# A fused attention and expert kernel on one core: the second dense group's preparation set later, the gate's last steps held back, two banks and the first loads rearranged

## The chip, the cores and the metric

The kernel runs on one NeuronCore of one Trainium2 chip. The metric is the time of one execution on the device in microseconds (us). TensorE (PE) multiplies, ScalarE (ACT) and VectorE (DVE) read its banks of PSUM and do the elementwise work, GpSimd (POOL) does elementwise work in SBUF and issues gathers and scatters, and SyncE (SP) issues most other transfers. Each engine works through its own instructions in order.

## The reference

Windowed attention, then a layer of eight experts of which each token takes two, then a dense layer with a piecewise gate. All in float32 (the second layer's weights come as float64 in the kernel's inputs and are decoded on the chip).

```python
rel = pos[:, None] - pos[None, :]
scores = np.where((rel >= 0) & (rel < 64), q @ k.T / 8, -1e9)
attn = exp(scores - max) / (sum + 1e-9)
x = (attn @ v)                                  # 2304 tokens x 512
noisy = x @ w_gate + log1p(exp(x @ w_noise)) * noise
top2 = the two largest of 8;  w = softmax over the two
x = sum over the two: w * (relu(x @ w1[e]) @ w2[e])          # 512 -> 1024 -> 512
h = x @ w_in                                                 # 512 -> 2048
g = where(h >= 1, h, where(h <= -1, 0, (h + 1) ** 2 / 4))
out = g @ w_out                                              # 2048 -> 512
```

## The kernel before

The tokens are cut into 18 tiles of 128. **Attention** goes by token tiles. The scores of tile i are two units u = 2i and 2i+1, each a bank of 128x512; units take the three banks `Sb` in turn (u modulo 3). `A` writes a tile's scores: two products with a mask open each bank, 32 products of queries and keys follow. `top` takes the row maxima on VectorE, `soft` the exponentials on ScalarE, `C` transposes the probabilities, and `Dm` multiplies them with the values into `OB`, a tile of two banks. Some filler products (`warm`) also go into `OB`. Before the loop SyncE is given the loads of keys and queries of the first pair of tiles (two halves), then values, then keys and queries of the second pair, then more values.

**Experts.** The tokens of an expert are gathered into tiles of 128 rows, transposed on TensorE (`xpose`, L756) into a bank, and copied out as a high half by ScalarE (L759) and a low half by VectorE (L760), since products run in a reduced form of float32 and three products of halves make one of full precision. A hidden chunk is 128 wide: `mm1` makes it (L885), ReLU leaves it in the hidden tile `hall` as two halves, and `mm2` (L949) adds its share to the output banks. Expert 0 comes in two parts, "0a" and "0b"; while 0b is worked on, the six tiles of the first large expert "e1" are transposed into bank 7, one per chunk, the last two at the same chunk. `tail` finishes the routing meanwhile, and `count` ranks the experts by their number of tokens.

**Dense layer.** The 18 tiles are cut into groups of 2, 4, 4, 4 and 4 (`G2`). The first group runs plainly (`plain`), while the others use a form with seven products of sums for eight (`wino`). In the first group the work goes in eight dense tiles p = 0 to 7, of two hidden chunks f = 0 and 1 each. For TensorE the order is: the first product of tile p+1 (L885, 24 products of 256 columns), then the second product of tile p (L949, 12 of 512 columns). Between lie the steps of `act_gate` for each chunk: ReLU (L903) and a half of it (L904) on ScalarE, two steps on VectorE (L905, L906), the copy into `hall` on ScalarE (L909) and the low half on VectorE (L910). The first product's banks 0 and 1 alternate by chunk.

The second group (called g1) is prepared while the first runs. For each of its four token tiles the two expert outputs y are loaded from `y_dram` through GpSimd's queue once all scatters have landed. They are scaled on ScalarE (L1019) and mixed on VectorE (L1021) in `mix_two`, transposed on TensorE in `xturn` (L1221) and copied by ScalarE in `xcopy` (L1227). `xsums` (L1240) forms the sums, and `split_two` (L1250, L1252) makes the halves of the seven operands. Where these steps stand is written out by hand: `FILL[(p, f)]` hangs steps into the gate of chunk f of tile p, and the main loop at the end of `fused_kernel` puts others between the seven steps j of a second product, by conditions on (p, j). The names y2 to y5 below are the second group's four token tiles, counted over all groups.

Of the kernel before, what the change touches and what calls it, by code (L numbers as in the profile page):

```python
# [11 lines left out]
F32 = mybir.dt.float32  # L12
# [19 lines left out]
NB = 5  # L32
# [25 lines left out]
def fused_kernel(ctx, tc, qT, kT, v, wg, noise, wcat, out, wd=None):  # L58
# [195 lines left out]
    load_qk(0)  # L254
    load_v(0)
    load_qk(1)
# [86 lines left out]

    def A(i):
        j = i // 2
        qo, ko = (i % 2) * P, (i % 2) * P
        sb = [Sb[(2 * i + k) % 3] for k in range(2)]
# [17 lines left out]
    def top(u):  # L365
        mx = wk.tile([P, 4], F32, tag="mx", name=f"mx{u}", bufs=3)
        nb = wk.tile([P, 4], F32, tag="nb", name=f"nb{u}", bufs=3)
        nc.vector.tensor_reduce(out=mx, in_=Sb[u % 3].rearrange("p (g n) -> p g n", g=4), axis=AX.X, op=ALU.max)
# [4 lines left out]
    def soft(u):  # L373
        sb, nb = Sb[u % 3], mxs.pop(u)
# [418 lines left out]
    def tail():  # L793
# [6 lines left out]
        count()  # L800
# [10 lines left out]
    def count():  # L811
# [25 lines left out]
                                in1=tf[:, 0:R].unsqueeze(2).to_broadcast([P, R, E]), op=ALU.is_equal)  # L837
        for a, src in enumerate((src_i, dst_i)):
# [59 lines left out]

    def act_gate(ps, hh, hl, w):
# [3 lines left out]
        nc.scalar.activation(r, ps, AF.Relu, bias=1.0)  # L903
        nc.scalar.activation(m, r, AF.Copy, scale=0.5)  # L904
        nc.vector.scalar_tensor_tensor(out=r, in0=m, scalar=1.0, in1=r, op0=ALU.min, op1=ALU.subtract)  # L905
        nc.vector.scalar_tensor_tensor(out=r, in0=m, scalar=1.0, in1=r, op0=ALU.min, op1=ALU.mult)  # L906
        for x in parts_of:
            next(x)
        nc.scalar.activation(hh, r, AF.Copy, scale=-1.0)  # L909
        nc.vector.scalar_tensor_tensor(out=hl, in0=r, scalar=-1.0, in1=hh.bitcast(F32), op0=ALU.mult, op1=ALU.subtract)  # L910
# [206 lines left out]
    def plain(ui, p):  # L1117
        w = wi[p % WS]
        for f in range(2):
# [6 lines left out]
            mm1_of(key, n, units[ui]["T"], act_gate, units[ui]["m1"], part(0), part(1))  # L1126
        load_in(p + WS)
# [130 lines left out]
    def copy_two(ui, b):  # L1258
        xcopy(ui, b)
        yield  # L1260

    def sums_two(ui, part):
        yield
        xsums(ui, part)

# [15 lines left out]
    for s in range(len(seq)):  # L1281
# [41 lines left out]
        def ahead_xpose():  # L1323
            for x, b, w in ahead:
                if f == (turn_at[b] if ui == WIDE - 1 else w + 2):
                    prep_xpose(x, b, bank[0] if ui == WIDE else TR)
# [48 lines left out]
        if ui == U7B and f:  # L1375
# [6 lines left out]
          {(5, 3): (6,)})  # L1382
    g1 = FIRST2 + 1

    def later(fn, *a):
        return lambda: fn(*a)
    FILL.update({(2, 1): [later(mix_two, units[g1], b) for b in (0, 1)],
                 (3, 0): [later(mix_two, units[g1], b) for b in (2, 3)],
                 (4, 0): [later(split_two, g1, 0), later(split_two, g1, 1)],
                 (4, 1): [later(sums_two, g1, (0, 1))],  # L1390
                 (5, 0): [later(sums_two, g1, (2, 3))],
                 (5, 1): [later(split_two, g1, j) for j in (2, 3)],
# [85 lines left out]
```

## Time and profile before

| | |
|---|---|
| median of 3 runs | 971.39 us (968.99 to 973.98) |
| profiled execution, its own time | 971.69 us |
| its span, first to last instruction | 969.9 us |
| TensorE busy | 944.0 us (97%) |
| VectorE busy | 661.6 us (68%) |
| ScalarE busy | 447.5 us (46%) |
| GpSimd busy | 220.2 us (23%) |
| mean granted TensorE clock | 0.994 |

The profile is one execution. A row of the order in time has the start, the duration, the engine, the line of the program, the operation, out<-in by the program's names without buffer numbers, the shapes, and in brackets how long the engine stood idle before it and what ended that. PEld is the weight load, which overlaps PE. SPq is SyncE's queue. Granted clock 1.00 means 2.4 GHz, 0.50 means 1.2 GHz.

### The profile page before, as it was taken

What the parts mean: (1) busy time and instruction counts of PE and PEld (TensorE: products, weight loads), DVE (VectorE), ACT (ScalarE), POOL (GpSimd) and SP (SyncE); (2) the same over time, 40 slices, a digit from 0 to 9 for tenths busy, and PEclk for the clock granted to TensorE, in tenths of its full rate; (3) what the DMA queues carried; (4) which work ended last, traced back from release to release, by engine and by line L of the source; (5) the groups of instructions that cost most, each with busy time, mean ns of one, the idle gap of its engine ahead of it and who ended that gap; (6) DMA issues with size and microseconds to landing.
All of it is one profiled execution on the core that took longest, in us unless ns stands there. A gap on an engine that the chain in (4) does not pass through costs nothing. (4 is left out here: it accounts for less than half of the span.)

```text
span 969.9 us, 18052 instructions
## 1 busy us (share of the span) xinstructions
PE 944.0 (97%) x6781; PEld 834.8 (86%) x6781; DVE 661.6 (68%) x1388; ACT 447.5 (46%) x920; POOL 220.2 (23%) x273
## 2 busy tenths in 40 slices
PE   8998999999999999999999997999999999999998
PEld 6886878988898989889888886898999889889897
DVE  4689565378997968889543365766766677577664
ACT  6897324345555555555432355334334333443222
POOL 3221113132634354254402130013002201300000
PEclk9999999999999999999999998999999999999999
DMA  8874125445878878757727574684576558546531
GB/s 249 296 266 144 56 97 187 178 167 192 291 257 290 260 244 278 254 196 251 252 82 239 178 234 159 200 298 155 174 249 230 173 174 295 165 161 214 189 106 44
DMA packets 91274, 196.95 MB, mean 203 GB/s; under 512 B 7320, under 2 KB 18072, under 8 KB 91184
## 3 DMA queue, kind: packets, MB, share of 16 engines
q1 hardware_dynamic: 83152, 171.68, 53.6%
q0 software_dynamic: 6736, 21.86, 6.3%
q10 hardware_dynamic: 1296, 2.23, 0.6%
q8 instruction: 54, 0.88, 0.4%
q14 instruction: 36, 0.29, 0.1%
HBM read 155.45 MB, written 40.29 MB: 202 GB/s over the span
## 5 line engine op out<-in xcount | busy, mean ns | idle before, releaser
L949 PE MATMUL bank<-wo,hall 128*128 128x512 f32 x864 | 239.5, 396 | 0.0
L949 PE MATMUL bank<-w,hall 128*128 128x512 f32 (+3 forms) x944 | 236.0, 398 | 1.4 <-DVE hall L896 1.3
L949 PEld LDWEIGHTS bank<-w,hall 128*128 128x128 f32 (+3 forms) x944 | 168.4, 184 | 37.0 <-DVE hall L896 1.7
L949 PEld LDWEIGHTS bank<-wo,hall 128*128 128x128 f32 x864 | 147.8, 190 | 17.5
L893 ACT ACTIVATE hall<-bank 128x288 fp32r<-128x288 f32 (+6 forms) x128 | 54.0, 422 | 223.3 <-PE bank L885 204.1
L885 PE MATMUL bank<-xhie,w 128*128 128x288 f32 (+4 forms) x768 | 123.0, 302 | 1.6 <-DVE hall L896 1.5
L885 PEld LDWEIGHTS bank<-xhie,w 128*128 128x128 f32 x768 | 113.9, 189 | 9.1 <-DVE hall L896 3.4
L896 DVE SCALAR_TENSOR_TENSOR hall<-bank,hall 128x288 fp32r<-128x288 f32 (+7 forms) x168 | 59.8, 391 | 87.2 <-ACT hall L893 78.5
L149 DVE TENSOR_TENSOR w<-raw,w 128x1024 fp32r<-128x1024 f32 (+1 forms) x71 | 82.4, 1160 | 24.4 <-ACT w L158 20.5
L1163 PEld LDWEIGHTS bank<-xb,wi 128*128 128x128 f32 x576 | 80.4, 188 | 11.5 <-DVE wg L1148 1.2
L1187 ACT ACTIVATE hall<-cg 128x512 fp32r<-128x512 f32 x64 | 40.3, 629 | 100.5 <-DVE cg L1185 100.5
L1163 PE MATMUL bank<-xb,wi 128*128 128x256 f32 x576 | 84.8, 283 | 1.8 <-ACT r L903 0.8
L1163 PEld LDWEIGHTS bank<-xc,wi 128*128 128x128 f32 x480 | 67.2, 188 | 7.6 <-DVE wg L1148 0.6
L1030 POOL TENSOR_TENSOR y<-y,y 128x512 f32<-128x512 f32 x14 | 19.1, 1363 | 227.2 <-ACT y L1029 227.2
L1163 PE MATMUL bank<-xc,wi 128*128 128x256 f32 x480 | 70.2, 281 | 0.2
L158 ACT ACTIVATE w<-raw 128x1024 fp32r<-128x1024 f32 (+1 forms) x71 | 69.3, 976 | 0.0
L885 PE MATMUL bank<-xloe,w 128*128 128x288 f32 (+4 forms) x384 | 69.0, 301 | 0.0
L204 POOL TENSOR_TENSOR td<-rawd 128x512 f32<-128x512 f32 x32 | 33.3, 1039 | 140.7 <-DVE rawd L202 78.2
L1181 ACT ACTIVATE mg<-cg 128x512 f32<-128x512 f32 x64 | 40.1, 626 | 47.1 <-DVE cg L1153 45.4
L1182 DVE SCALAR_TENSOR_TENSOR cg<-mg,cg 128x512 f32<-128x512 f32 x64 | 47.0, 734 | 18.8 <-ACT mg L1181 18.8
L885 PEld LDWEIGHTS bank<-xloe,w 128*128 128x128 f32 x384 | 58.0, 188 | 0.0
L1191 DVE SCALAR_TENSOR_TENSOR hall<-cg,hall 128x512 fp32r<-128x512 f32 x64 | 45.9, 718 | 9.1 <-ACT hall L1187 8.7
(279 smaller groups left out, 1443.5 us busy)
## 6 DMA issues: line engine op xcount, KB each, us to landing
wi<-w1o SPq DMA_DIRECT2D x56, 1024.0 KB
raw<-wcat SPq DMA_DIRECT2D x64, 512.0 KB
rawd<-wd SPq DMA_DIRECT2D x32, 512.0 KB
w1o<-so SPq DMA_DIRECT2D x64, 256.0 KB
y<-y_dram SPq DMA_DIRECT2D x28, 256.0 KB
vE<-v SPq DMA_DIRECT2D x18, 260.0 KB
x_dram<-x SPq DMA_DIRECT2D x18, 256.0 KB
k<-kT SPq DMA_DIRECT2D x8, 512.0 KB
```

Source lines behind the costliest of these rows:

```text
L149: nc.vector.tensor_tensor(out=w[:, 1, c], in0=t[:, c], in1=w[:, 0, c].bitcast(F32), op=ALU.subtract)
L158: nc.scalar.activation(w[:, 0, c], t[:, c], AF.Copy)
L204: nc.gpsimd.tensor_tensor(out=t, in0=hf, in1=lf, op=ALU.add)
L885: nc.tensor.matmul(ps, lhsT=l[k], rhs=r[:, k, s:s + w], start=(c == 0), stop=(c == len(prods) - 1))
L893: nc.scalar.activation(hh, ps, AF.Relu)
L896: nc.vector.scalar_tensor_tensor(out=t, in0=ps[:, c], scalar=0.0, in1=hh[:, c].bitcast(F32), op0=ALU.max, op1=ALU.subtract)
L949: nc.tensor.matmul(M2[b][0:w], lhsT=h2[:, o:o + w], rhs=r[n], start=(first and a == 0), stop=(last and a == end))
L1163: nc.tensor.matmul(ps, lhsT=w[:, l, k * P:k * P + P], rhs=r[:, m, k, :], start=(c == 0), stop=(c == len(prods) - 1))
L1181: nc.scalar.activation(st["m"], c, AF.Relu, scale=0.5)
L1182: nc.vector.scalar_tensor_tensor(out=c, in0=st["m"], scalar=1.0, in1=c, op0=ALU.min, op1=ALU.subtract)
L1187: nc.scalar.activation(h2[:, 0:T], c, AF.Copy, scale=-1.0)
L1191: nc.vector.scalar_tensor_tensor(out=h2[:, T:2 * T], in0=c, scalar=-1.0, in1=h2[:, 0:T].bitcast(F32), op0=ALU.mult, op1=ALU.subtract)
```

## The change

Six things, all of them in the order or the place of work; no arithmetic is added or taken away.

1. The keys and queries of the second pair of tiles are loaded ahead of the first values.
2. The second unit of the second token tile (u = 3) puts its scores into the first bank of `OB` instead of `Sb[0]`.
3. `count` gains a yield before its last part, and `tail` passes it on.
4. The last two steps of `act_gate` (ScalarE's copy into `hall`, VectorE's low half) are held in a list and issued by `close_gate` behind the next chunk's ReLU; behind the last tile they are issued at once.
5. The sixth tile of e1 is transposed into bank 4 instead of bank 7.
6. The second dense group is prepared later: mixing in tiles 3 and 4 instead of 2 and 3, transposes and copies in the second products of tiles 3 and 4 instead of 2, sums in tile 4's, splits in tiles 5 to 7.

```diff
     load_qk(0)
+    load_qk(1)
     load_v(0)
-    load_qk(1)
...
+    def score(u):
+        return OB[:, 0, :] if u == 3 else Sb[u % 3]
...
-        sb = [Sb[(2 * i + k) % 3] for k in range(2)]
+        sb = [score(2 * i + k) for k in range(2)]
...
+    held_gate = []
+
+    def close_gate():
+        for r, hh, hl in held_gate:
+            nc.scalar.activation(hh, r, AF.Copy, scale=-1.0)
+            nc.vector.scalar_tensor_tensor(out=hl, in0=r, scalar=-1.0, in1=hh.bitcast(F32), op0=ALU.mult,
+                                           op1=ALU.subtract)
+        held_gate.clear()
...
         nc.scalar.activation(r, ps, AF.Relu, bias=1.0)
+        close_gate()
...
+        held_gate.append((r, hh, hl))
         for x in parts_of:
             next(x)
-        nc.scalar.activation(hh, r, AF.Copy, scale=-1.0)
-        nc.vector.scalar_tensor_tensor(out=hl, in0=r, scalar=-1.0, in1=hh.bitcast(F32), op0=ALU.mult, op1=ALU.subtract)
...
+        if p == NPR - 1:
+            close_gate()
...
-                    prep_xpose(x, b, bank[0] if ui == WIDE else TR)
+                    prep_xpose(x, b, bank[0] if ui == WIDE else bank[4] if ui == WIDE - 1 and b == NB else TR)
...
-          {(5, 3): (6,)})
+          {})
+    TURN, COPY = {(3, 0): (0,), (3, 1): (1,), (3, 6): (2,), (4, 0): (3,)}, {(3, 3): (0, 1), (4, 2): (2, 3)}
...
-    FILL.update({(2, 1): [later(mix_two, units[g1], b) for b in (0, 1)],
-                 (3, 0): [later(mix_two, units[g1], b) for b in (2, 3)],
-                 (4, 0): [later(split_two, g1, 0), later(split_two, g1, 1)],
-                 (4, 1): [later(sums_two, g1, (0, 1))],
-                 (5, 0): [later(sums_two, g1, (2, 3))],
-                 (5, 1): [later(split_two, g1, j) for j in (2, 3)],
-                 (6, 0): [later(split_two, g1, j) for j in (4, 5)]})
+    FILL.update({(3, 0): [later(mix_two, units[g1], 0)],
+                 (3, 1): [later(mix_two, units[g1], 1)],
+                 (4, 0): [later(mix_two, units[g1], b) for b in (2, 3)],
+                 (5, 0): [later(split_two, g1, j) for j in (0, 1)],
+                 (6, 0): [later(split_two, g1, j) for j in (2, 3)],
+                 (6, 1): [later(split_two, g1, j) for j in (4, 5)],
+                 (7, 0): [later(split_two, g1, 6)]})
...
+                    for b in TURN.get((p, j), ()):
+                        xturn(ui + 1, b)
+                    for b in COPY.get((p, j), ()):
                         xcopy(ui + 1, b)
+                    if p == 4 and j > 4:
+                        xsums(ui + 1, (0, 1) if j == 5 else (2, 3))
```

How the instructions stand now is shown at three places. A row has the line, the operation, out<-in with buffer numbers, and the shape.

ScalarE, the gates of the first group where y is scaled, before (r and m are a chunk's gate, r_7017 is chunk 1 of tile 2, r_7056 chunk 0 of tile 3):

```order
L903 ACTIVATE r_7017<-bank1_74 128x256
L904 ACTIVATE m_7018<-r_7017 128x256
L1019 ACTIVATE y2_6963<-y2_6963,wts_189 128x512
L1019 ACTIVATE y3_6966<-y3_6966,wts_189 128x512
L909 ACTIVATE hall_2150<-r_7017 128x256
L903 ACTIVATE r_7056<-bank0_73 128x256
L904 ACTIVATE m_7057<-r_7056 128x256
L1019 ACTIVATE y4_6970<-y4_6970,wts_189 128x512
L1019 ACTIVATE y5_0_6974<-y5_0_6974,wts_189 128x512
L909 ACTIVATE hall_2150<-r_7056 128x256
```

And now (r_7050 is chunk 0 of tile 3, r_7072 its chunk 1, r_7109 chunk 0 of tile 4; L916 is the ReLU, L907 the held copy):

```order
L916 ACTIVATE r_7050<-bank0_73 128x256
L907 ACTIVATE hall_2150<-r_7015 128x256
L918 ACTIVATE m_7051<-r_7050 128x256
L1032 ACTIVATE y2_6961<-y2_6961,wts_189 128x512
L916 ACTIVATE r_7072<-bank1_74 128x256
L907 ACTIVATE hall_2150<-r_7050 128x256
L918 ACTIVATE m_7073<-r_7072 128x256
L1032 ACTIVATE y3_6964<-y3_6964,wts_189 128x512
L916 ACTIVATE r_7109<-bank0_73 128x256
L907 ACTIVATE hall_2150<-r_7072 128x256
L918 ACTIVATE m_7110<-r_7109 128x256
L1032 ACTIVATE y4_6968<-y4_6968,wts_189 128x512
```

y2 moved by one chunk, y3 to y5 by two, and each copy into `hall` now stands behind the next chunk's ReLU and no longer behind a y of its own chunk.

TensorE, where the y tiles are transposed, before (wo2 is the weight of tile 2's second product, wi0 that of tile 4's first):

```order
L885 MATMUL bank1_74<-xlog0_6798,wi3_6554 128x256 x4
L1221 MATMUL bank7_78<-idn_164,y2_6963 128x128 x4
L949 MATMUL bank2_75<-wo2_6739,hall_2150 128x512
L1221 MATMUL bank4_2142<-idn_164,y3_6966 128x128 x4
L949 MATMUL bank2_75<-wo2_6739,hall_2150 128x512 x2
L949 MATMUL bank3_76<-wo2_6739,hall_2150 128x512 x3
L949 MATMUL bank2_75<-wo2_6739,hall_2150 128x512 x2
L1221 MATMUL bank5_77<-idn_164,y4_6970 128x128 x4
L949 MATMUL bank2_75<-wo2_6739,hall_2150 128x512
L949 MATMUL bank3_76<-wo2_6739,hall_2150 128x512
L1221 MATMUL bank6_2143<-idn_164,y5_1_6975 128x128 x4
L949 MATMUL bank3_76<-wo2_6739,hall_2150 128x512 x2
```

And now (the rows above these hold the whole second product of tile 2 and the first product of tile 4; y5 follows after the first product of tile 5):

```order
L889 MATMUL bank1_74<-xlog0_6798,wi0_6347 128x256 x4
L1236 MATMUL bank7_78<-idn_164,y2_6961 128x128 x4
L962 MATMUL bank2_75<-wo3_6774,hall_2150 128x512
L1236 MATMUL bank4_2142<-idn_164,y3_6964 128x128 x4
L962 MATMUL bank2_75<-wo3_6774,hall_2150 128x512 x2
L962 MATMUL bank3_76<-wo3_6774,hall_2150 128x512 x3
L962 MATMUL bank2_75<-wo3_6774,hall_2150 128x512 x3
L962 MATMUL bank3_76<-wo3_6774,hall_2150 128x512
L1236 MATMUL bank5_77<-idn_164,y4_6968 128x128 x4
```

The transposes moved down by one second product and one first product of a dense tile.

ScalarE at the group's start, before (r_6882 is chunk 1 of tile 0, y7b the last expert's outputs, wo6 and wo7 weight splits, r_6932 chunk 0 of tile 1):

```order
L904 ACTIVATE m_6883<-r_6882 128x256
L909 ACTIVATE hall_2150<-r_6882 128x256
L966 ACTIVATE y7b_0_6896<-bank4_2142 128x512
L955 ACTIVATE y7b_2_6909<-bank6_2143 32x512
L1111 ACTIVATE wo6_6914<-wr6_6777 128x1024
L1111 ACTIVATE wo7_6917<-wr7_6816 128x1024
L903 ACTIVATE r_6932<-bank0_73 128x256
```

And now (r_6880 is chunk 1 of tile 0, r_6930 chunk 0 of tile 1):

```order
L918 ACTIVATE m_6881<-r_6880 128x256
L979 ACTIVATE y7b_0_6894<-bank4_2142 128x512
L968 ACTIVATE y7b_2_6907<-bank6_2143 32x512
L1124 ACTIVATE wo6_6912<-wr6_6777 128x1024
L1124 ACTIVATE wo7_6915<-wr7_6816 128x1024
L916 ACTIVATE r_6930<-bank0_73 128x256
L907 ACTIVATE hall_2150<-r_6880 128x256
```

The copy of tile 0's chunk 1 into `hall` moved from ahead of the two evictions to behind the two weight splits and the next ReLU; VectorE's low half moved in the same way.

## Rows read from the trace of the kernel before

**Rows 1.** What TensorE waited for, whole span: us in total, times, longest us.
```profile
PE bank L1221 <- DVE y L1021: 5.5, 1, 5.5
PE bank L352 <- ACT p L377: 1.9, 2, 1.0
PE bank L756 <- DVE xloe L760: 1.8, 2, 1.5
```

**Rows 2.** Order in time, first dense group, ScalarE's y and TensorE's transposes.
```profile
581.61 0.72 ACT L1019 ACTIVATE y<-y,wts 128x512 f32<-128x512 f32 x1 [2.48 <-DMA y<-y_dram]
...
585.06 0.72 ACT L1019 ACTIVATE y<-y,wts 128x512 f32<-128x512 f32 x1 [2.73 <-DMA y<-y_dram]
...
587.26 1.12 PE L1221 MATMUL bank<-idn,y 128*128 128x128 f32 x4 [5.53 <-DVE y L1021]
...
587.85 0.72 ACT L1019 ACTIVATE y<-y,wts 128x512 f32<-128x512 f32 x1 [0.37 <-DMA y<-y_dram]
...
594.48 1.07 PE L885 MATMUL bank<-xhig,wi 128*128 128x256 f32 x8
```

**Rows 3.** Stretches: their us, busy us by engine, granted clock, DMA share, GB/s.
```profile
170.00:171.00 1.00, 1.00 (x4) 0.79 (x3) 0.45 (x2) 0.95 (x1) 0.00 (x0) 0.50 0.13 53
...
585.00:586.00 1.00, 0.00 (x0) 0.00 (x0) 0.00 (x0) 0.94 (x3) 0.00 (x0) 1.00 1.03 381
...
591.00:592.00 1.00, 1.00 (x3) 0.73 (x3) 0.66 (x2) 0.27 (x1) 0.00 (x0) 0.50 0.00 0
```

**Rows 4.** Order in time, TensorE from expert 0b to the first large expert.
```profile
160.83 0.46 PE L756 MATMUL bank<-idr,xge 128*128 128x128 f32 x4
161.13 1.63 PE L949 MATMUL bank<-w,hall 128*128 128x512 f32 x6
162.59 1.10 PE L885 MATMUL bank<-xhi0b,w 128*128 128x256 f32 x8
...
169.08 0.50 PE L756 MATMUL bank<-idr,xge 64*128 64x64 f32 x4 [1.46 <-DVE xloe L760]
...
174.49 1.44 PE L885 MATMUL bank<-xhie,w 128*128 128x352 f32 x8
...
176.41 1.56 PE L949 MATMUL bank<-w,hall 128*128 128x512 f32 x6
```

**Rows 5.** Order in time, first 15 us; last, a wait of SyncE's queue.
```profile
9.13 0.41 PE L352 MATMUL bank<-mask,id 64*64 64x512 bf16 x2 [0.95 <-ACT p L377]
...
10.93 0.51 SPq L108 DMA_DIRECT2D qbuf<-qT  x1
...
11.03 0.60 ACT L386 ACTIVATE pt<-bank 128x512 f32<-128x512 f32 x1 [0.92 <-PE bank L384]
...
12.71 0.40 PE L352 MATMUL bank<-mask,id 64*64 64x512 bf16 x2 [0.94 <-ACT p L377]
...
14.50 0.27 PE L398 MATMUL ob<-vE__120,pt 128*64 128x65 f32 x1
...
SPq L409 <- DMA qbuf<-qT: 0.9, 1, 0.9
```

**Rows 6.** Order in time, start and end of the first dense group.
```profile
565.38 2.02 PE L949 MATMUL bank<-w,hall 128*128 128x512 f32 x8
...
568.36 0.58 ACT L966 ACTIVATE y7b<-bank 128x512 f32<-128x512 f32 x1
...
570.07 2.92 PE L949 MATMUL bank<-wo,hall 128*128 128x512 f32 x12
...
570.54 2.36 DVE L1112 TENSOR_TENSOR wo<-wr,wo 128x1024 fp32r<-128x1024 f32 x2 [0.27 <-ACT wo L1111]
...
574.48 1.00 PEld L885 LDWEIGHTS bank<-xhig,wi 128*128 128x128 f32 x8 [0.28 <-ACT r L903]
...
615.85 0.97 PE L1163 MATMUL bank<-xb,wi 128*128 128x256 f32 x6 [0.79 <-ACT r L903]
...
617.93 0.98 PE L1163 MATMUL bank<-xb,wi 128*128 128x256 f32 x6 [0.64 <-ACT sg L1144]
```

More of the change, by code (lines that the diff above doesn't have):

```diff
@@ L367, in top @@
         nb = wk.tile([P, 4], F32, tag="nb", name=f"nb{u}", bufs=3)
-        nc.vector.tensor_reduce(out=mx, in_=Sb[u % 3].rearrange("p (g n) -> p g n", g=4), axis=AX.X, op=ALU.max)
+        nc.vector.tensor_reduce(out=mx, in_=score(u).rearrange("p (g n) -> p g n", g=4), axis=AX.X, op=ALU.max)
         (nc.vector if u < 4 else nc.gpsimd).tensor_scalar(out=nb, in0=mx, scalar1=-0.125, scalar2=None, op0=ALU.mult)
@@ L373, in soft @@
     def soft(u):
-        sb, nb = Sb[u % 3], mxs.pop(u)
+        sb, nb = score(u), mxs.pop(u)
         p = wk.tile([P, 4, P], F32, tag="p", name=f"p{u}", bufs=4)
@@ L799, in tail @@
         prep_gather(units[1], 0)
-        count()
+        yield from count()
         rte.close()
@@ L837, in count @@
                                 in1=tf[:, 0:R].unsqueeze(2).to_broadcast([P, R, E]), op=ALU.is_equal)
+        yield
         for a, src in enumerate((src_i, dst_i)):
@@ L1256, in xsplit @@
             pass
[L1258 to L1264, printed above, removed]
     SPLITS = {0: [int(F0 <= f < F0 + NF - EW) for f in range(NF)], 1: [0] + [1] * (NF - 1),
@@ L1431, in fused_kernel @@
                         xcopy(ui + 1, 2 * (p - 2) + j // 2)
-                elif p == 2:
-                    if j in (0, 1, 5, 6):
-                        xturn(ui + 1, j if j < 2 else j - 3)
-                    for b in {3: (0, 1), 6: (2, 3)}.get(j, ()):
+                else:
+                    for b in TURN.get((p, j), ()):
+                        xturn(ui + 1, b)
+                    for b in COPY.get((p, j), ()):
                         xcopy(ui + 1, b)
+                    if p == 4 and j > 4:
+                        xsums(ui + 1, (0, 1) if j == 5 else (2, 3))
                 for x in AT[late].get((p, j), ()):
```

## The prediction

> **What bounds the kernel now.** I read the waits of TensorE first, then the order in time around its long waits, then the granted clock there. The page shows TensorE busy nearly throughout, so what can be won lies in the few places where it stands idle or runs slowly. The list of its waits names them [rows 1]: one of 5.5 us for a token tile y, mixed on VectorE, two for the exponentials, together 1.9, and two for the low half of a transposed tile, together 1.8, of which one is 1.5.
>
> The long one is in the first dense group. The y tiles of the second group are loaded from GpSimd's queue, after the last scatter. ScalarE takes the first at 581.61, the second at 585.06 and the last at 587.85, each when it lands [rows 2]. ScalarE works in order, so all that stands behind these tiles waits too; TensorE reaches the first transpose of y 5.53 us before it can run it, at 587.26. The idle time is not the whole price. The granted clock was still full between 585 and 586, but 0.50 from 591 to 592: it had gone from 2.4 to 1.2 GHz [rows 3]. The next dense tile's first product, at 594.48, comes late on both counts.
>
> The same shows on a smaller scale at the first expert [rows 4, 3]: its last two tiles are transposed into one bank, the second waits 1.46 us for VectorE to empty it, and the clock is 0.50 from 170 to 171. At the kernel's start [rows 5] the second token tile's scores wait 0.95 us for a bank that ScalarE still reads. ScalarE then idles 0.92 us, to 11.03, before the first copy of transposed probabilities.
>
> **The change part by part.** The sum is made against the profiled execution's own 971.69 us, which stands 0.3 above the median of 971.39.
>
> *Last transpose of the first expert, into bank 4.* The wait of 1.46 goes: bank 4 is free there, since the expert that uses it has been evicted and the next writes it only after this tile is copied. The slow stretch: from 169.08 to 174.49 are 5.41 us, for one short transposition, six products of 512 columns and twelve of 352. At full clock these took 0.30 (160.83 to 161.13), 1.46 (161.13 to 162.59) and 1.92 (174.49 to 176.41), so 3.68 [rows 4]. Lost to the clock: 1.73. Term: **-3.19**. What is late next is the copy pair of the last tile on ScalarE and VectorE; both can now run right behind the fifth tile's, while TensorE has six products of 1.46 us to do. Bounds: 1.46 (the clock falls all the same) to 3.19.
>
> *Second group prepared about one dense tile later.* The same transposes, mixes, copies and splits run, none more, none fewer; SyncE's and GpSimd's queues keep their order there, so the tiles land as before. In the order above the first scaling of y now stands behind the ReLU of dense tile 3, and the first transpose behind the products of tile 4. Without the stall TensorE needs about 5.9 us from 581.73 (587.26 less 5.53) to get there (twelve products of 512, 2.92, and tile 4's 24 of 256, about as long), so 587.6. The second y lands at 585.06 and needs a scaling and a mix of about 0.7 each (ScalarE's took 0.72), 586.5: a margin of 1.1. The fourth has until tile 5 is multiplied, over 6 us more, against 587.85. Therefore the 5.53 goes. Slow clock: from 587.26 to 594.48 are 7.22 us for four transposes (1.2) and twelve products (2.92), so 3.10 lost. Term: **-8.63**. Bounds: if the y tiles come 2 us later than now, TensorE waits 0.9 us and may slow again (1.7), so -6.0; nothing more is there to win.
>
> *The held gate.* The last two steps of a chunk's gate (ScalarE's copy into the hidden tile, VectorE's low half) now stand behind the next chunk's ReLU. That frees the score bank sooner, and the 0.28 us that TensorE waited for a ReLU at 574.48 goes [rows 6]: **-0.28**. Against it: the second chunk of each tile is closed only after the next tile's first chunk is multiplied. TensorE multiplies that tile before it consumes the closed chunk, and consumes the other chunk first (six products, 1.46), so there is room. It is tightest at the first tile, where two evictions and two weight splits stand between. As they ran before, VectorE's splits end at 572.90 (570.54 and 2.36) and the low half behind them would end at 573.3; TensorE starts on that tile at 570.07 and is due there eight products later, at 572.0: 1.3 late. But ScalarE took the first of these evictions at 568.36, behind the gate's copy that now stands after it, though TensorE was done with the tiles to evict by 567.4 (565.38 and 2.02) [rows 6]. That brings evictions and splits forward by 1 to 1.5 us. I take the wait as nothing, since the two are about equal; the bound above is 1.3, and 1.7 more with a slow clock behind it.
>
> At the end of the group TensorE waits 0.79 and 0.64 us, for the last ReLU and for the first copy of the next form of product [rows 6]. The first goes, since the ReLU is now ahead of the chunk before it. The second grows by as much, since the last chunk's chain of five steps is no shorter and a split of x (about 0.7 on each engine, as the scaling of y) has moved in ahead of it. Taken as nothing; bounds -0.8 to +0.6.
>
> *Second tile's late scores in a value bank.* TensorE need not wait the 0.95 at 9.13. ScalarE then has its next work as soon as the exponentials of the first tile end (10.11), against 11.03: at most 0.92 sooner. I take 0.75, since the scores must still be transposed and copied in turn. The following tile's wait of 0.94 at 12.71 stays, since it is for ScalarE, and moves with it. The first value products write the same bank, at 14.50 now, 13.75 then; the exponentials that read it end as much sooner. Between here and the first expert no long wait stands in rows 1, so a start that is earlier stays earlier. Term: **-0.75**; bounds 0 and -0.92.
>
> *Second keys and queries ahead of the values.* Two loads move ahead of two others in SyncE's queue. SyncE had issued the next queries by 11.44 (10.93 and 0.51) and then waited 0.9 us on the second queries [rows 5]: they landed at about 12.34. The third tile's scores want them at about 12.0 after the edit above, so without the swap a third of a microsecond is lost again. The values land at 12.34 at the latest if the four together take what they took, and are first read at 13.75. The third keys and queries are issued up to 1.3 us later, some 10 us ahead of use. Nothing of its own; it keeps the term above whole. The Trainium skill, page "DMA: Bandwidth & Descriptors", section "Queues, rings and completion order", says that a queue's descriptors are consumed in ring order on each engine, but that a later one may finish before an earlier one. By its first half the term stays 0.75; by its second the queries may still come at 12.34 and it would be 0.4, the sum 959.2.
>
> *The rest.* The new yield in the counting routine moves no row on any engine: nothing.
>
> Sum: 3.19 + 8.63 + 0.28 + 0.75 = 12.85, so 971.69 - 12.85 = **958.8 us**.
>
> **The rivals.** *The clock falls at the end of the group instead.* The two waits there become one of about 1.5 us, as long as the one at the first expert, behind which the clock fell (1.73 lost). For it: the length. Against it: 1.43 us in two pieces left the clock at full today. It would give 958.8 + 1.7 = 960.5. The Trainium skill, page "TensorE: Matmul & The Clock Gate", Part 1, says that slow is the default, that activity lifts it, and that where the change falls differs from run to run; by that rule equal waits may end differently, and 960.5 would be as likely as 958.8. The rows alone, one fall behind a wait in one piece and none behind two short ones, I read as 0.18.
>
> *The wait moves and doesn't go.* The y tiles land later than now, since TensorE, no longer stalled, has the next weights ordered sooner; the margin of 1.1 at the second transpose is used up. At 2 us late: 0.9 of wait and 1.7 of slow clock, 961.4. Against it: the weights of that step are ordered at about 587.5, when all but the last tile are in.
>
> *Values late.* The first value products wait for their tile, which now stands behind 1 MB of keys and queries. At 1.5 us late the early term turns to +0.75: 960.3.
>
> *Slower: the held gate is late at every tile.* If VectorE's closing half ends after TensorE has done the first six products and two more, TensorE waits in each of the eight dense tiles. From 1.6 us each (8 x 1.6 = 12.8) this eats the gain; at 2.0 with the clock halved twice it gives 958.8 + 16 + 3.4 = 978. For it: at the first tile there is no margin. Against it: from the second on no weight split stands between, and the closing is due 2.9 us after the ReLU's bank is ready, for about 1.3 us of work.
>
> **How the numbers follow.** Forecast 0.60; clock at the group's end 0.18; wait moved 0.10; values late 0.07; slower 0.02; a start or an expert term that isn't kept (961 to 967) 0.03. The range runs from 955.8 (the group's end also gains, and runs differ by about 2 either way) to 963.5, which takes in the first three rivals with the same spread. About 0.5%, 4.9 us, is what a measurement of this kernel can tell from no change; faster by more means under 966.5. Only the last cases miss it, or several at once: faster 0.92, same 0.06, slower 0.02.
>
> **What would show it.** In the profile after: no wait of TensorE for y and none for the low half at the first expert; granted clock 1.00 in the stretches that answer to rows 3; the second tile's scores in one piece, ScalarE's first copy at about 10.1; one wait of some 1.5 us in place of the two at the end of the group. Wrong it would be if a transpose of y still waited, if the clock fell without a wait, or if products on hidden tiles waited for VectorE's closing half.

## The result, and the profile after

| | before | after |
|---|---|---|
| median | 971.39 us (five runs, 968.99 to 973.98) | 957.97 us (five runs, 957.70 to 958.46) |
| profiled execution | 971.69 us | 958.46 us |
| its span | 969.9 us | 956.8 us |
| TensorE busy | 944.0 us | 938.8 us |
| mean granted clock | 0.994 | 1.000 |

The ratio is 0.9864, with a 95% interval of 0.9847 to 0.9881. The forecast was 958.8. Both falls of the clock are gone, and so is most of the spread: the runs of after lie within 0.8 us, those of before within 5.

TensorE's waits after the change (engine, bank and line, what is waited for: total, times, longest) are short:

```profile
PE bank L889 <- DVE hall L900: 1.5, 3, 1.1
PE bank L962 <- DVE hall L900: 1.3, 1, 1.3
...
PE bank L355 <- ACT p L380: 0.9, 1, 0.9
...
PE bank L1178 <- ACT sg L1159: 0.9, 1, 0.9
PE bank L759 <- DMA xg0a<-x_dram,src_i: 0.8, 1, 0.8
...
PE bank L364 <- DMA qbuf<-qT: 0.4, 1, 0.4
PE bank L759 <- POOL y L1043: 0.4, 1, 0.4
```

The waits for y's mixing and for the low half of e1 [rows 1] aren't in the list any more. The first two rows shown, for hidden halves of the experts, stand in the list of before too, with 1.5 and 1.3. No row is for L908, the held low half of the dense gate. Three others are new and small: for a gather (xg0a), for queries and for a mixed y tile at the dense stage's start.

The places that the leads below are counted from, in the profile before (mask products of the first tile, fifth tile of e1, dense tile 0, dense tile 6, and the first product on xa; xa and xb are operands of the next form of product, the one on sums):

```profile
5.44 0.56 PE L352 MATMUL bank<-mask,id 64*64 64x512 bf16 x4
...
167.17 0.46 PE L756 MATMUL bank<-idr,xge 128*128 128x128 f32 x4
...
562.55 1.10 PE L885 MATMUL bank<-xhig,wi 128*128 128x256 f32 x8
...
605.53 1.11 PE L885 MATMUL bank<-xhig,wi 128*128 128x256 f32 x8
...
620.15 0.88 PE L1163 MATMUL bank<-xa,wi 128*128 128x256 f32 x6
```

The first dense group in the order in time, ScalarE and TensorE after the change:

```profile
558.72 1.10 PE L889 MATMUL bank<-xhig,wi 128*128 128x256 f32 x8
...
577.44 0.73 ACT L1032 ACTIVATE y<-y,wts 128x512 f32<-128x512 f32 x1 [0.23 <-DMA y<-y_dram]
...
579.76 0.72 ACT L1032 ACTIVATE y<-y,wts 128x512 f32<-128x512 f32 x1 [0.70 <-DMA y<-y_dram]
...
582.70 1.33 ACT L1032 ACTIVATE y<-y,wts 128x512 f32<-128x512 f32 x2
...
583.01 0.60 PE L1236 MATMUL bank<-idn,y 128*128 128x128 f32 x4
...
593.10 1.11 PE L889 MATMUL bank<-xhig,wi 128*128 128x256 f32 x8
```

The first two y tiles are still waited for, but by ScalarE alone (0.23 and 0.70). The first transpose, at 583.01, has no bracket: it doesn't wait. The first product of tile 6, 605.53 in the profile before, starts at 593.10, so 12.43 earlier; the first of tile 0 starts 3.83 earlier (558.72 against 562.55). The granted clock (the figure before the last two columns) is full where rows 3 show falls:

```profile
166.00:167.00 1.00, 1.00 (x7) 0.88 (x8) 0.77 (x2) 1.00 (x4) 0.00 (x0) 1.00 0.31 53
...
587.00:588.00 1.00, 1.00 (x10) 0.96 (x9) 0.00 (x0) 0.00 (x0) 0.00 (x0) 1.00 0.64 246
605.00:606.00 1.00, 1.00 (x8) 0.95 (x8) 0.45 (x2) 0.00 (x0) 0.00 (x0) 1.00 1.06 412
```

TensorE at the first large expert after the change, which answers to rows 4:

```profile
165.49 0.89 PE L759 MATMUL bank<-idr,xge 128*128 128x128 f32 x8
166.31 1.65 PE L962 MATMUL bank<-w,hall 128*128 128x512 f32 x6
...
171.65 1.56 PE L962 MATMUL bank<-w,hall 128*128 128x512 f32 x6
```

The two tiles are transposed in one piece. The six products that end rows 4 at 176.41 start at 171.65 now: 4.76 earlier, of which 1.68 had been won before (the tiles started at 167.17 and start at 165.49). So 3.08 were won here.

The kernel's start, TensorE and ScalarE after:

```profile
4.85 0.41 PE L355 MATMUL bank<-mask,id 64*64 64x512 bf16 x4
...
7.84 0.29 PE L364 MATMUL bank<-k,qbuf 64*64 64x128 f32 x1 [0.40 <-DMA qbuf<-qT]
...
9.57 0.60 ACT L389 ACTIVATE pt<-bank 128x512 f32<-128x512 f32 x1
...
13.07 0.27 PE L401 MATMUL ob<-vE,pt 128*64 128x65 f32 x1
```

The wait of 0.95 [rows 5] is gone, and ScalarE's first copy is at 9.57 instead of 11.03. The mask products start 0.59 earlier as well (before: 5.44), with nothing changed for TensorE ahead of them; the profiles below show the same spread in kernels with and without the first two parts.

And the end of the group, TensorE and ScalarE after:

```profile
604.01 0.42 ACT L907 ACTIVATE hall<-r 128x256 fp32r<-128x256 f32 x1 [1.00 <-DVE r L920]
604.34 0.37 ACT L1159 ACTIVATE sg<-bank 128x256 f32<-128x256 f32 x1
...
604.76 0.98 PE L1178 MATMUL bank<-xb,wi 128*128 128x256 f32 x6 [0.92 <-ACT sg L1159]
...
606.97 0.88 PE L1178 MATMUL bank<-xa,wi 128*128 128x256 f32 x6
```

One wait of 0.92 stands where rows 6 have 0.79 and 0.64. From tile 6 to the product at 604.76 another 0.74 us was won: it was at 617.93 before, 13.17 later, against 12.43 at tile 6.

### The profile page after: what moved, and what is told of

It is laid out like the page before. It is cut to its first block, busy times and chain, and to the rows that moved or that the text cites. A ratio compares the mean times of both kernels' runs of the same rounds, so it can differ in the third digit from the quotient of the medians.

```text
span 956.8 us, 18056 instructions
## 1 busy us (share of the span) xinstructions
PE 938.8 (98%) x6781; PEld 831.4 (87%) x6781; DVE 660.7 (69%) x1388; ACT 445.7 (47%) x920; POOL 220.6 (23%) x273
```

## The experiments

The runs went in three batches, each on one chip beside the kernel before, whose medians were 970.49 (31 runs), 970.45 (7) and 969.62 (7). The changed kernel itself stands in the third only. Where a run of another batch is set against it below, the chips differ, and its median is 957.97 in the result's runs and 957.33 in the third batch.

The dense group can also be measured by itself, from the first product of tile 0 to the first product on xa. It took 57.60 us in the profile before, 52.54 with the held gate alone, 51.54 with the late preparation alone, 51.69 in the changed kernel without the held gate, and 48.25 to 48.27 in the six profiles that have both as the change has them (the changed kernel twice, and the versions below that differ from it in the start, in bank 7 or in GpSimd's mix). Behind that product all the profiles named here take the same 349.7 to 349.8 us to the end.

**The late preparation alone** (the tables and the main loop of the sixth part, on the kernel before):

```diff
-    FILL.update({(2, 1): [later(mix_two, units[g1], b) for b in (0, 1)],
...
+    FILL.update({(3, 0): [later(mix_two, units[g1], 0)],
+                 (3, 1): [later(mix_two, units[g1], 1)],
...
```

> The kernel before with the sixth part alone: the second dense group is mixed, transposed, copied and split later; each gate keeps its last two steps where they were. My account: the wait of 5.53 us for y goes and the clock stays at 1.00 behind it, 8.6 us less in the first dense group, 971.4 - 8.6 = 962.8; the waits of 0.28, 0.79 and 0.64 for the ReLUs and the first copy of the next form stay. Rival: the later order only works with the held gate, since each scaling of y now stands ahead of a chunk's copy into the hidden tile; then TensorE waits for hidden tiles in two or three dense tiles, about 1 us each and perhaps 1.7 of slow clock, 965 to 968.

Measured: 965.64 us (ratio 0.9957, 0.9941 to 0.9973), 4.9 less than before and not 8.6. In its profile (964.58, the second fastest of its ten runs) the stall for y is gone, as expected, and from tile 0 to tile 6 the group is 8.26 us shorter. But at the end of the group TensorE lost 2.2 us of that again. ScalarE and TensorE there, with the granted clock of a stretch behind it:

```profile
607.23 0.42 ACT L909 ACTIVATE hall<-r 128x256 fp32r<-128x256 f32 x1 [1.24 <-DVE r L906]
...
607.97 1.49 PE L1163 MATMUL bank<-xb,wi 128*128 128x256 f32 x6 [1.69 <-ACT r L903]
```

```profile
610.00:611.00 1.00, 1.00 (x4) 0.73 (x4) 0.74 (x2) 0.22 (x1) 0.00 (x0) 0.50 0.01 2
```

The wait for the last ReLU, 0.79 before, is 1.69, and the clock is at 1.2 GHz behind it. That ReLU stands behind the copy of the chunk before, and the copy waited 1.24 us for VectorE, whose steps of that chunk stood behind two splits of x. My account fell: the later order needs the held gate, though not where the rival looked for it: the products on hidden tiles (L949) wait 1.3 us in all, as before.

**The held gate alone** (the fourth part, on the kernel before):

```diff
         nc.scalar.activation(r, ps, AF.Relu, bias=1.0)
+        close_gate()
...
+        held_gate.append((r, hh, hl))
...
-        nc.scalar.activation(hh, r, AF.Copy, scale=-1.0)
-        nc.vector.scalar_tensor_tensor(out=hl, in0=r, scalar=-1.0, in1=hh.bitcast(F32), op0=ALU.mult, op1=ALU.subtract)
...
```

> The kernel before with the fourth part alone: the last two steps of each gate stand behind the next chunk's ReLU. My account after seeing the whole change: the 0.28 us wait for a ReLU goes, and at the end of the group the waits of 0.79 and 0.64 become one of about 0.9, so about 0.8 to 1.0 us less in all, 970.5; the wait for y stays at about 5.5 with its slow clock. My forecast's account: the end of the group gains nothing, one wait of about 1.5, so 0.3 less, 971.1. Rival that would make it slower: the second product waits in each of eight tiles for VectorE's closing half, over 0.5 us each, 975 or more.

Measured: 966.30 us (0.9966, 0.9952 to 0.9980), 4.2 less: four times what any of my accounts gave it. The profile of before has the reason, in rows that I had not read. ScalarE and VectorE before, behind the y scaled at 585.06 [rows 2]:

```profile
585.69 0.40 ACT L909 ACTIVATE hall<-r 128x256 fp32r<-128x256 f32 x1
...
586.12 0.43 DVE L910 SCALAR_TENSOR_TENSOR hall<-r,hall 128x256 fp32r<-128x256 f32 x1 [6.07 <-ACT hall L909]
586.46 1.41 DVE L1021 SCALAR_TENSOR_TENSOR y<-y,wts 128x512 f32<-128x512 f32 x2
```

The first y was scaled by 582.33 and could have been mixed then. But VectorE's mix stood behind a low half, which waited 6.07 us for ScalarE's copy, which stood behind the scaling of the *second* y. Holding the gate's last steps back takes copy and low half out of that chain. The held kernel, ScalarE, VectorE and TensorE at the same place:

```profile
581.71 0.72 ACT L1028 ACTIVATE y<-y,wts 128x512 f32<-128x512 f32 x1 [3.77 <-DMA y<-y_dram]
...
582.47 0.75 DVE L1030 SCALAR_TENSOR_TENSOR y<-y,wts 128x512 f32<-128x512 f32 x1 [3.58 <-ACT y L1028]
...
583.27 0.65 PE L1232 MATMUL bank<-idn,y 128*128 128x128 f32 x4 [1.07 <-DVE y L1030]
...
585.46 1.12 PE L1232 MATMUL bank<-idn,y 128*128 128x128 f32 x4 [1.30 <-DVE y L1030]
```

The first y lands at the same time (581.71, before 581.61), yet its transpose runs at 583.27 instead of 587.26. Two waits of 1.07 and 1.30 stay, where each y is waited for itself; the clock still fell behind them, to 0.50 from 586 to 588. In this profile 4.29 us are won from tile 0 to tile 6 and 0.77 from there to the first product on xa.

**The changed kernel without the held gate:**

```diff
-        close_gate()
...
-        held_gate.append((r, hh, hl))
...
+        nc.scalar.activation(hh, r, AF.Copy, scale=-1.0)
+        nc.vector.scalar_tensor_tensor(out=hl, in0=r, scalar=-1.0, in1=hh.bitcast(F32), op0=ALU.mult, op1=ALU.subtract)
...
```

> The changed kernel without the held gate: each gate's last two steps stand in its own chunk again. My account: with the second group prepared late there is no long wait for y to shorten, so the hold is worth only the end of the group: there the last ReLU stands behind copies and a split of x again and TensorE waits about 1.7 us for it, as with the later preparation alone, and the clock may fall behind it (1.5 to 1.7 more). So 957.8 + 0.3 + 1.0 to 2.8, that is 959.1 to 960.9, and runs spread over more than a microsecond. Rival, the forecast's: 0.3 at one ReLU and nothing at the end, 958.1. Rival, that the hold alone carries about 4 us as it did on the kernel before: 962.

Measured: 961.97 us (0.9916, 0.9889 to 0.9943), 4.0 above after's first median, at the size of the last rival, though not for its reason: there is no stall for y. Its profile lost 3.44 us to the changed one between the dense stage's start and the first product on xa, 0.33 of it to tile 6 and 3.11 at the place that the late preparation alone had shown; another 1.0 it had lost before the dense stage, where the hold has no part. TensorE there:

```profile
606.17 1.22 PE L1167 MATMUL bank<-xb,wi 128*128 128x256 f32 x6 [1.70 <-ACT r L907]
```

Behind this wait the clock fell too, to 0.50 from 607 to 610. But two of the four runs (961.99 and 960.46) have a recorded clock of 1.000, so the fall is not what they lost by. So the hold is worth about 4 us either way in the times, and 5.06 and 3.44 in the group of the two profiles: with the old order it shortens the stall for y, with the new one it keeps the group's end from stalling. The parts don't add up one by one (5.06 and 6.06 alone, 9.35 together): they share the stall for y, and the late order makes a stall that the hold removes.

**Bank 4 alone**, on the kernel before:

```diff
-                    prep_xpose(x, b, bank[0] if ui == WIDE else TR)
+                    prep_xpose(x, b, bank[0] if ui == WIDE else bank[4] if ui == WIDE - 1 and b == NB else TR)
```

> The kernel before with the fifth part of the change alone: the sixth tile of the first large expert is transposed into bank 4. My account: TensorE's wait of 1.46 us for VectorE's low half goes, and with it the slow stretch behind it, so that the stretch from that transposition to the last product of 352 columns takes about 3.2 us less; granted clock 1.00 in it; nothing given back before the first dense group, so the time is 971.4 - 3.2 = 968.2. Rival A: the clock falls there anyway, since the chunk of six transpositions is uneven: then 1.5 us less and a clock of 0.50 still, 969.9. Rival B: the experts are held by their loads and gathers, and about a third of it is given back by the time the dense layer starts, as the profile of the whole change suggests (0.9 us given back there): 969.1, with the waits that take it behind the last scatter of the large experts.

Measured: 969.06 us (0.9984, 0.9970 to 0.9997), 1.4 less: rival B's figure. Wait and slow stretch are gone, as in my account, and by the six products that end rows 4 its profile is 3.04 us ahead of before's. At the last y tile of the first dense group it is 0.35 ahead (559.92 against 560.27), and its stall for the second group's y is 6.0 instead of 5.5. This profile, 971.79, is the slowest of its ten runs, so it shows how the gain can be lost and not how much of it is. About half of what the expert stage gained went in waits at y tiles, of 0.39 us for a mixed y and 1.14 us for a tile's low half whose engines had waited for y. A part went so in the changed kernel's first profile too: 4.76 ahead at e1, it was 3.83 ahead when the dense stage began.

**Bank 7 again, in the changed kernel** (the reverse of that edit):

```diff
-                    prep_xpose(x, b, bank[0] if ui == WIDE else bank[4] if ui == WIDE - 1 and b == NB else TR)
+                    prep_xpose(x, b, bank[0] if ui == WIDE else TR)
```

> The changed kernel with the sixth tile of the first large expert back in bank 7, all else as changed. My account: a wait of about 1.5 us for VectorE's low half returns in every run, and the clock falls behind it in some runs and not in others (it fell in two of four profiles with that wait): so the runs fall into two heaps, about 1.0 to 1.5 and 2.7 to 3.2 us above 957.8, with a granted clock that is lower in the second. Rival: the clock always falls, one heap at about 961. Rival: most is taken up at the start of the dense stage, where tiles are waited for that come at a time of their own: under 0.7 above 957.8.

Measured: 960.76 us (0.9912, 0.9885 to 0.9939), four runs from 960.11 to 962.15, 2.8 above after's first median and 3.4 above its second. So without the stall that absorbs it, the term is worth about its 3.19. These four runs make one heap, not two, with a granted clock of 0.997 or 0.998. TensorE there, and the clock of a stretch:

```profile
166.94 0.50 PE L759 MATMUL bank<-idr,xge 64*128 64x64 f32 x4 [1.46 <-DVE xloe L763]
167.37 2.63 PE L962 MATMUL bank<-w,hall 128*128 128x512 f32 x6
...
168.00:169.00 1.00, 1.00 (x4) 0.71 (x3) 0.48 (x2) 0.80 (x1) 0.00 (x0) 0.50 0.08 33
```

The kernel with the late preparation alone has the same wait and the same six products:

```profile
169.03 0.50 PE L756 MATMUL bank<-idr,xge 64*128 64x64 f32 x4 [1.45 <-DVE xloe L760]
169.45 1.66 PE L949 MATMUL bank<-w,hall 128*128 128x512 f32 x6
...
170.00:171.00 1.00, 1.00 (x6) 0.81 (x5) 0.48 (x2) 0.89 (x1) 0.00 (x0) 1.00 0.08 33
```

A wait of 1.46 and 2.63 us for the products; a wait of 1.45 and 1.66: the first fell to 1.2 GHz and the second didn't. Of the five profiles with this wait, all of 1.45 or 1.46, the clock fell in three (before, 2.83 us for the products; the first two parts alone, 2.08; this one) and not in two (1.66 in the late preparation alone and in the held gate alone).

**The first two parts alone**, on the kernel before:

```diff
     load_qk(0)
+    load_qk(1)
     load_v(0)
-    load_qk(1)
...
+        return OB[:, 0, :] if u == 3 else Sb[u % 3]
...
```

> The kernel before with the first two parts: second keys and queries loaded ahead of the first values, and the second tile's late scores in a value bank. My account: TensorE's wait of 0.95 us goes, ScalarE's first copy of transposed probabilities comes 0.75 to 0.9 us sooner than the mask products would put it, and TensorE reaches the first large expert 0.75 to 1.1 us sooner: 970.5. The filler products at the start took 3.45 us in the profile of the whole change and 4.04 before; if that comes from this change it shows here again and the start gains 1.4 to 1.7, 969.8; if it is a matter of when the clock rises in a run, it differs among these four profiles without regard to the edit. Rival: the first value products wait for values that now stand behind 1 MB of keys and queries: no gain, 971.4 or more.

Measured: 970.10 us (0.9997, 0.9978 to 1.0015): no difference that the times tell. In the profile the first value products come 8.08 us after the mask products; before it is 9.06. Its stall for y is 4.2 us long, with the order of before.

**The changed kernel with the old order of loads**, the scores still in the value bank:

```diff
     load_qk(0)
+    load_v(0)
     load_qk(1)
-    load_v(0)
```

> The changed kernel with the second keys and queries loaded behind the first values again, as before; the late scores stay in the value bank. Forecast's account: the third tile's scores wait a few tenths of a microsecond for their queries, 0.3 to 0.4 of the early start is lost: 958.2. Rival: the loads are there in time in either order, 957.9. Rival: the wait falls where ScalarE is waited for anyway and only the first two products of the value tiles move: 957.9 too, told from the second by a wait for the queries in the list.

Measured: 958.09 us (0.9887, 0.9866 to 0.9907); from masks to value products 8.84 us, with no wait for queries in the list. One profile; see the next.

**The changed kernel without its first two parts** (both edits undone as shown above):

> The changed kernel without its first two parts: loads in the old order, the second tile's late scores in the old bank. My account: the wait of 0.95 us returns and the first value products come 0.8 to 1.0 us later; without a stall further on that could absorb it, 0.8 to 1.1 is lost: 958.8. Rival: a wait for a gather at the first expert (0.8 us in the profile of the changed kernel, 0 to 0.4 in others) takes most of it up: 958.1.

**The changed kernel once more**, unchanged:

> The changed kernel once more, on this chip, to compare the others with: 957.9 within 0.5, a granted clock of 1.00 and runs within 1 us of each other; the kernel before spreads over 3 us or more, in heaps of granted clock (0.994, 0.996, 0.998), if the clock's falls behind its two long waits are what spreads it.

Measured in the same batch: 957.85 (0.9885, 0.9866 to 0.9905) without the first two parts and 957.33 (0.9876, 0.9859 to 0.9893) with them, the latter's four runs between 956.12 and 957.63. The half microsecond is within the intervals, and those four runs lie 1.5 us apart, not within 1. The profiles tell more. From the first mask product to the first value product it took 8.93 to 9.22 us in the five profiles without these parts; with both, 7.97 to 8.26 in six of eight, and 8.67 and 8.95 in the other two. What these two lost, and the profile with the old order of loads (8.84), can be seen. TensorE with the old order of loads, with bank 7 and with both small edits further down:

```profile
5.87 1.65 PE L364 MATMUL bank<-k,qbuf 64*64 64x128 f32 x32
```

```profile
12.05 1.10 PE L364 MATMUL bank<-k,qbuf 64*64 64x128 f32 x32 [0.56 <-DMA qbuf<-qT]
```

```profile
5.87 1.55 PE L364 MATMUL bank<-k,qbuf 64*64 64x128 f32 x32
```

The first tile's 32 score products took 1.65 and 1.55 us in two of them, 1.04 to 1.10 in all other profiles; the order of loads isn't what sets them apart, since one has the old and one the new. In the third (8.95) the third tile's scores waited 0.56 us for their queries, which were loaded ahead of the values. Counted from the filler products behind the first tile's scores, it is 7.69 to 7.97 us in the five profiles without these parts, 6.70 to 7.00 in seven of the eight with both, and 6.83 with the value bank and the old order of loads. So the early term is there, some 0.95 us, but other things move the start by as much. The mask products themselves start between 4.72 and 5.45 us, whatever the kernel: behind the same nine filler products, which took 3.45 us in after's profile and 4.04 in before's at a granted clock of 1.00 in both.

This second profile of after (span 954.4) also has neither of the small new waits of the first, for a gather and for the y tiles of the dense stage's start, and is 2.36 us ahead of it when the dense stage begins. So these waits come and go from one execution of the same kernel to the next.

**The closing steps behind the next form's first copy**, an attempt to go on from the changed kernel:

```diff
-        if p == NPR - 1:
-            close_gate()
...
                 next(gen)
+            close_gate() if (ui, p, j) == (FIRST2, NPR - 2, 0) else None
```

> The changed kernel with the last chunk's closing copy and low half issued behind the first copy of the next form of product instead of ahead of it. My account: that copy then runs as soon as ScalarE is free, at about 603.0 instead of 604.34, and TensorE's wait of 0.92 us at the end of the group goes: 957.1, 0.8 less. Rival: another wait takes its place (VectorE's steps or the bank of the next product), no difference: 957.8.

Measured: 956.64 us (0.9875, 0.9844 to 0.9907). ScalarE and TensorE:

```profile
601.74 0.36 ACT L1157 ACTIVATE sg<-bank 128x256 f32<-128x256 f32 x1
602.85 0.42 ACT L907 ACTIVATE hall<-r 128x256 fp32r<-128x256 f32 x1 [0.74 <-DVE r L920]
...
602.50 0.87 PE L1176 MATMUL bank<-xb,wi 128*128 128x256 f32 x6
...
604.11 0.98 PE L1176 MATMUL bank<-xb,wi 128*128 128x256 f32 x6 [0.27 <-DVE cg L1166]
```

The copy (sg) runs first now, the wait of 0.92 is gone, and one of 0.27 behind it takes some of that: the group is 0.63 us shorter (47.62 from tile 0 to the first product on xa). The times don't tell it from the changed kernel's.

**The first dense group's y mixed on VectorE** instead of GpSimd:

```diff
             nc.scalar.activation(y1, y1, AF.Copy, scale=wts[:, t, 0:1])
+            if un is units[FIRST2]:
+                nc.vector.scalar_tensor_tensor(out=y2, in0=y2, scalar=wts[:, t, 1:2], in1=y1, op0=ALU.mult, op1=ALU.add)
+                gat[un["key"], b] = y2
+                return
```

> The changed kernel with the first dense group's two y tiles mixed as the second group's are: one scaling on ScalarE and one multiply-and-add on VectorE (0.7) in place of two scalings on ScalarE and an addition of 1.29 us on GpSimd. My account: the chain from landing to transposition is about 1.3 us shorter, TensorE's two waits there (some 0.9 us together, by which the dense stage starts less early than the expert stage ends early) go, and about 0.6 to 0.9 is gained: 957.1. Rival: VectorE is late with the low halves of hidden tiles there, and the time is the same or 0.5 more: 957.8 to 958.3.

Measured: 956.69 us (0.9870, 0.9844 to 0.9895). No wait for y there; but the second profile of after has none either, so the edit is not shown to do anything.

**Both together:**

> Both small edits together on the changed kernel: the closing steps behind the first copy of the next form of product, and the first dense group's y mixed on ScalarE and VectorE. Each gave about 1.2 us alone against 957.9, in traces 0.8 at the group's end and 1.0 at the dense stage's start. My account: they lie in different places and both on TensorE's path, so they add: 955.4 to 956.1, with TensorE never waiting as long as 1.0 us there. Rival: what the earlier start of the dense stage gains is taken back by y tiles of the second group that are not earlier: 956.6, no better than either alone.

Measured: 957.43 us (0.9879, 0.9858 to 0.9900), beside 957.33 of the changed kernel on the same chip. The account of both, 955.4 to 956.1, missed. No version is shown to beat the changed kernel: the 0.6 to 0.7 us that the first edit saves in the traces (0.63 and 0.66) are below what these runs can tell.

## Why the prediction was right

The forecast was 0.8 us above the median and 0.3 above the profiled execution. Its main steps held, and smaller ones were mis-sized. That the sum came so near is partly luck. Between the two profiles the span fell by 13.1, and five pieces that the forecast had at nothing make up 0.65 of it: mask products 0.59 earlier, 0.86 more by the first expert's first tile (most of it a late start told of below), 0.74 at the end of the group, less 0.61 from there to e1's fifth tile (a gather was waited for 0.84) and 0.93 from e1 to the dense stage. The second profile of after lies 2.4 us lower without any edit, and the stall that the largest term is read from was 5.5, 6.0 and 4.2 us long in the three profiles with that order of before.

- **Second group later, -8.63, and the ReLU wait of 0.28.** Together 8.91 for the group; the two profiles give 8.60 from the dense stage's start (3.83 earlier) to tile 6 (12.43 earlier). Each can be seen alone: without the hold the late order gives 8.26 and 8.27 there, and the hold adds 0.33. The step "the tiles land as before" was off, without harm: counted from tile 0's first product, ScalarE took the first y tile after 18.7 us (19.1 before) and the second after 21.0 (22.5 before). The second was mixed by 581.27 (its row on VectorE starts at 580.52 and takes 0.75) and transposed at 583.69, so the margin was 2.4 and not 1.1, and the tight case was not put to the test. But the step's view of the stall was incomplete. "All that stands behind these tiles waits too" was true of VectorE as well, and most of what the first transpose waited for was VectorE's own order, not the landing of its y. The sum didn't suffer, since a later preparation removes either cause.
- **Held gate, -0.28.** As a term of the whole it was mis-sized: taken out of the changed kernel, the hold costs about 4.0 in the times and 3.44 in the group's profiles. Two effects were left out: the mix that no longer stands behind the low half, and the end of the group, where I compared with the waits of the old order (0.79 and 0.64) and not with those that the late splits of x would make there (1.69, and a slow clock). The step there, "the second grows by as much", failed too: one wait of 0.92 and 0.74 us won, not 0, near the edge of its bounds (-0.8 to +0.6).
- **Bank 4, -3.19.** The two profiles give 3.08; put back in the changed kernel, the old bank costs 2.8 to 3.4. On the kernel before it was worth 1.4; that the waits for y took the rest is seen in one slow profile only.
- **Second tile's scores, -0.75, and keys first.** Some 0.95 in the profiles, at the bound of 0.92, but not measurable in the times. Whether the order of loads is needed for it stays open. In the one profile without it TensorE didn't wait for queries, but the third tile's scores came late there (12.60), behind the slow scores of the first; in one profile with it (bank 7 again) TensorE waited 0.56 us for them all the same.
- **The yield, 0.** It wasn't tried alone; VectorE's rows of the counting routine stand in the same order in both profiles. A late start that the forecast had no row for went with the change: at the end of attention VectorE starts on the value products' bank 0.77 to 0.80 us after the last of them in four of the five profiles made from the kernel before, and 0.04 to 0.05 us after it in all nine with the other parts in place. VectorE before, and in the second profile of after:

```profile
98.49 0.17 DVE L403 TENSOR_SCALAR rl<-ob 128x8 f32<-128x8 f32 x1 [2.07 <-PE bank L384]
```

```profile
96.04 0.17 DVE L406 TENSOR_SCALAR rl<-ob 128x8 f32<-128x8 f32 x1 [1.35 <-PE ob L401]
```

  In the fifth profile, of the late preparation alone, the clock fell at that very place instead (0.50 from 97 to 98). The order of instructions there is the same in all of them. Its cause is open.
- **The rivals.** The clock didn't fall at the group's end; the wait there was 0.92 and not 1.5. With 1.69 and 1.70, in the kernels without the hold, it fell in both profiles, so that rival was near, though not in every run of them. The wait for y didn't move to another place. Values weren't late: no profile's list has a wait of TensorE for them. The held gate was in time at the first tile: VectorE's low half there ended at 567.93, and TensorE's products of the tile ran from 566.23 without an idle bracket.

## What to carry to other kernels

When a wait names the engine that ends it, follow that engine's own queue back past the row it names: here ready work stood behind a step that waited for a later transfer, and moving two steps was worth half of what the stall cost. Cost each part of a change against the kernel that the other parts leave, since a part may be worth nothing, or four microseconds, by what stands beside it. A wait of TensorE costs its length or, where the clock fell behind it, more: taking away waits of 5.53 and 1.46 us gave 8.26 and 3.08 here. And measure a stage by itself where its kernel's other stages are noisy: the dense group repeated within 0.02 us in six profiles whose spans differ by up to 4.7.

## What the runs showed that I had not expected

The same wait of 1.45 to 1.46 us before the same products left the clock at 2.4 GHz in two kernels' profiles and let it fall to 1.2 in three others', and the six products behind it took 1.66 us in the two and 2.08 to 2.83 in the three. The Trainium skill, page "TensorE: Matmul & The Clock Gate", Part 1, says that where the change to full speed falls differs from run to run; it says so of the rise, and these five profiles show the like of the fall. A part of the spread of the kernel before goes with the clock recorded for each run: of its 31 runs in one batch, six with a granted clock of 0.998 took 968.2 to 969.2 us, nine with 0.994 took 970.0 to 972.9, and one with 0.991 took 977.3. But the fifteen between, at 0.995 and 0.996, took 967.9 to 972.4, so it is not all. With the long waits gone the spread is smaller and not gone: nine runs of the changed kernel lie between 956.12 and 958.46, but in four of its variants, whose profiles show no wait of TensorE above 1.3 us, the slowest run took 959.1 to 959.8.
